# Two-branch gated mix on one core: subtractions and products of the feature maps move from VectorE to GpSimd, 131 instead of 130 packs of softmax exponentials on VectorE, and a new planned order

## The chip, the cores and the metric

The kernel runs on one core of a Trainium2 chip. Its engines are TensorE (PE; matmuls, and PEld for the loads of their weights), VectorE (DVE), ScalarE (ACT), GpSimd (POOL) and SyncE (SP, which here only issues DMAs). The metric is the device time of one execution in microseconds; the kernel before takes 737.42 us, the median of 3 runs (737.13 to 737.89).

## The reference

Two attention branches share the input `x` (2048 tokens, 512 features, 32 heads of 16) and are mixed by a gate of each token:

```python
x = A_x
g = _sigmoid((x * gate_w).sum(-1, keepdims=True))
# branch A: softmax attention
q, k, v = split(x @ A_wqkv)                       # 32 heads of 16
p = softmax(einsum("bhqd,bhkd->bhqk", q, k) * 16 ** -0.5)
a = (p @ v) @ A_wo
# branch B: linear attention with "hedgehog" feature maps
q, k, v = split(x @ B_wqkv)
pq, pk = q @ w_phi, k @ w_phi                     # 16x16 per head
phi_q = concat([softmax(pq), softmax(-pq)])       # 32 features
phi_k = concat([softmax(pk), softmax(-pk)])
kv = einsum("bhsf,bhsd->bhfd", phi_k, v);  z = phi_k.sum(over s)
b = (einsum("bhqf,bhfd->bhqd", phi_q, kv) / (phi_q . z + 1e-6)) @ B_wo
return g * a + (1 - g) * b
```

Branch A needs 2048 x 2048 x 32 exponentials. They are the bulk of the work.

## The kernel before, in words

**Units, packs, groups.** A unit is one head, 128 keys and 512 queries: one score matmul into a PSUM bank (128 x 512) and one exponential of it. Four units of four heads make a pack (512 packs in all), 16 packs (all keys) a group, of which there are 32, eight for each of the four stretches of 512 queries.

**Two ways to an exponential.** Most units go to ScalarE: `_qk` (the matmuls of `_scores`, L1131) fills 2 or 3 banks of a ring of five, and `_exp` (L1183) makes the exponentials of these 2 or 3 banks in one instruction, into `ET`. The packs named in `AWAY` (one number for each group; bit n stands for key block 1 + 3n, and bit 5, if it were set, for pack 510, the second last of all) go to VectorE: `_vector_bits` turns each of the four score banks into a bit pattern (L962, `va`, "v_bits"), and `_vector_terms` makes three shifted copies out of it that stand for a sum of powers of two; the first is `va` itself or a shift of it on VectorE (L984, `vp`, "v_term", one or two packs in one instruction), and the third is made by GpSimd in two halves (`_pool_term`, L999, "p_term"). `_values` (L1250) multiplies `ET`, or the terms, with the values. A vector pack costs 12 such matmuls where a pack of ScalarE costs 4. `_fill` (L1257) adds zeros where PE would otherwise run dry.

**End of a group.** `_norm` moves the accumulated 128 x 512 tile out of PSUM by a transpose (L1271, "n_t1", into `T1`) and, after every second group, makes the factor from the softmax's denominator and the gate (L1278 on GpSimd, L1280), multiplies (L1282, "n_mul", from `T1` into `T2`) and sends the result through two DMAs (`turned`, then `onTA`) to the output matmuls. The last group has a function of its own, `_norm_last`, which works by halves.

**Branch B.** It is worked off beside the attention, by four token tiles of 128 at a time (`_b_quad`, called eight times: four for the keys, four for the queries). Each call projects (L651, L1395), finds the greatest and the least of each head's 16 values by a tree (L1414, "b_max"), subtracts each from the values (L1423, "b_sub", two instructions of 128 x 2048 in a quad), lets ScalarE make the two exponentials (L1425, "b_exp"), sums them (L1430, L1432, and L1434 on GpSimd) and scales one side by a ratio (`_b_scale`: L1447 to L1455, of which "b_mul", 128 x 2048, is L1450 for keys and L1455 for queries). The keys' product is read by the `kv` matmuls (L1473), the queries' by transposing DMAs (L1511).

**What sets the order.** The order on each engine is fixed when the program is built. Every operation is given to a planner (`Plan.op`) with an engine, a cost and a due time (`prio`); `Plan.order` places them one by one, first what can start earliest, then what is due first, and writes one list for each engine. `SHIFT` moves the due times of tagged groups of operations by up to 14 packs. Operations named in `PORT` and all of GpSimd's are placed so that they don't overlap: each GpSimd operation is made to wait for the latest VectorE operation of that kind, while VectorE is not made to wait for GpSimd's. Each engine then works its list strictly in order and waits at each entry for semaphores. ScalarE's list holds the exponentials of both branches, so an L1425 whose input is late stops the L1183 behind it.

Of the kernel before, what the change touches and what calls it, by code (L numbers as in the profile page):

```python
# [7 lines left out]
ALU = mybir.AluOpType  # L8
AX = mybir.AxisListType

P = 128
# [378 lines left out]
class _Kernel:  # L390
# [364 lines left out]
    def _gate(self):  # L755
# [44 lines left out]
    AWAY = (26, 27, 26, 31, 22, 13, 15, 15, 31, 15, 13, 31, 30, 23, 31, 15, 29, 31, 26, 27, 31, 26, 31, 21, 31, 31, 28, 31, 31, 11, 23, 31)  # L800

    SHIFT = (
# [582 lines left out]
    def _b_quad(self, s, t0, due):  # L1385
# [22 lines left out]
        def run(name, cost, fn, at, reads, writes):  # L1408
            eng = "POOL" if name in ("b_ratio", "b_tot") else "DVE"
            op(eng, fn, cost, reads=reads, writes=writes, name=name, prio=due + gap * at)  # L1410
# [259 lines left out]
```

## Time and profile before

| | |
|---|---|
| median of 3 runs | 737.42 us (737.13 to 737.89) |
| profiled execution | 737.4 us, of which the span of the profile is 735.6 us |
| granted TensorE clock | 1.000 |
| PE, DVE, ACT, POOL busy | 713.1, 690.5, 723.5, 303.8 us |
| exponentials of branch A on ACT | 304 of 128 x 1536, 303 of 128 x 1024, a few smaller |
| score tiles turned by DVE (L962) | 520, which is 130 packs |

Busy time is the time in which at least one instruction of the engine was running; instructions of one engine overlap by their ends, so the mean durations times the count exceed the busy time. "Idle before" and the waits name what an engine waited for. Times within the profile count from the span's start.

### The profile page before, as it was taken

What the parts mean: (1) busy time and instruction counts of PE and PEld (TensorE: products, weight loads), DVE (VectorE), ACT (ScalarE), POOL (GpSimd) and SP (SyncE); (2) the same over time, 40 slices, a digit from 0 to 9 for tenths busy, and PEclk for the clock granted to TensorE, in tenths of its full rate; (3) what the DMA queues carried; (4) which work ended last, traced back from release to release, by engine and by line L of the source; (5) the groups of instructions that cost most, each with busy time, mean ns of one, the idle gap of its engine ahead of it and who ended that gap; (6) DMA issues with size and microseconds to landing.
All of it is one profiled execution on the core that took longest, in us unless ns stands there. A gap on an engine that the chain in (4) does not pass through costs nothing.

```text
span 735.6 us, 19777 instructions
## 1 busy us (share of the span) xinstructions
PE 713.1 (97%) x8549; PEld 234.4 (32%) x8549; DVE 690.5 (94%) x1085; ACT 723.5 (98%) x636; POOL 303.8 (41%) x318
## 2 busy tenths in 40 slices
PE   8999999999999999999999999999999999999998
PEld 3334233243223223332232233333332233332322
DVE  4899999988999999999999999999999999999996
ACT  6999999999999999999999999999999999999996
POOL 3832342424544424535353344334334444344442
PEclk9999999999999999999999999999999999999999
DMA  9400100001010010100001032042123111003210
GB/s 201 145 10 6 22 2 9 16 4 18 4 15 11 4 20 2 17 11 8 14 2 17 15 61 28 8 83 35 23 45 74 21 16 23 16 25 63 40 29 30
DMA packets 90041, 21.96 MB, mean 30 GB/s; under 512 B 82913, under 2 KB 89441, under 8 KB 89953
## 3 DMA queue, kind: packets, MB, share of 16 engines
q1 hardware_dynamic: 88752, 20.30, 14.5%
q8 instruction: 67, 1.10, 0.7%
q10 hardware_dynamic: 1200, 0.39, 0.2%
q14 instruction: 22, 0.17, 0.1%
HBM read 4.21 MB, written 2.10 MB: 9 GB/s over the span
## 4 chain that ended last, share of the span: by engine, by line
ACT 73%; PE 13%; DVE 11%; DMA 1%; issue 0%; POOL 0%; DVEq 0%; POOLq 0%
ACT ET L1183 70%; PE ps L1131 5%; DVE va L962 4%; PE ps L1250 4%; ACT bq L1425 3%; PE ps L651 2%; DVE vp L984 2%; DVE btree L1414 1%; DMA xT<-in_A_x_dram 1%; PE ps L744 1%; PE ps L1257 1%; DVE bq L1423 0%; DVE VB L1541 0%; DVE nb L1541 0%; DVE rb L1539 0%
## 5 line engine op out<-in xcount | busy, mean ns | idle before, releaser
L1183 ACT ACTIVATE ET<-ps 128x1536 bf16<-128x1536 f32 (+1 forms) x612 | 692.9, 1343 | 4.6 <-PE ps L1131 4.4
L999 POOL TENSOR_SCALAR vp<-va 128x1024 uint16<-128x1024 uint16 x264 | 275.7, 1044 | 337.3 <-DVE vp L984 124.2
L962 DVE TENSOR_SCALAR va<-ps 128x512 uint16<-128x512 f32 x520 | 339.5, 681 | 23.9 <-PE ps L1131 21.7
L1131 PE MATMUL ps<-qT,kT 32*128 32x512 bf16 (+1 forms) x2053 | 311.0, 384 | 10.1 <-ACT ET L1183 5.1
L1131 PEld LDWEIGHTS ps<-qT,kT 32*128 32x128 bf16 x2053 | 82.7, 91 | 258.3 <-ACT ET L1183 146.5
L984 DVE TENSOR_SCALAR vp<-va 128x4096 uint16<-128x4096 uint16 (+1 forms) x151 | 162.0, 1079 | 0.6 <-PE ps L1250 0.2
L1250 PE MATMUL ps<-ET,V 128*32 128x512 bf16 x1532 | 149.0, 385 | 1.3 <-DVE T L1271 1.0
L1250 PE MATMUL ps<-vp,vc 128*32 128x512 bf16 x1040 | 93.9, 384 | 0.3 <-DVE vp L984 0.2
L1250 PEld LDWEIGHTS ps<-ET,V 128*32 128x32 bf16 x1532 | 39.3, 95 | 64.9 <-issue 48.6
L651 PE MATMUL ps<-WB,xT 128*32 128x512 bf16 x768 | 57.4, 382 | 0.5 <-DVE bq L1395 0.3
L1250 PE MATMUL ps<-va,V 128*32 128x512 bf16 x520 | 51.3, 385 | 0.0
L1250 PE MATMUL ps<-vp,V 128*32 128x512 bf16 x520 | 48.2, 383 | 0.3 <-DVE vp L984 0.2
L1257 PE MATMUL ps<-kT,zero 128*32 128x512 bf16 x468 | 42.1, 384 | 0.0
L651 PE MATMUL ps<-xT,WA 128*32 128x512 bf16 x480 | 36.1, 382 | 0.6 <-DVE va L962 0.4
L1250 PEld LDWEIGHTS ps<-vp,vc 128*32 128x32 bf16 x1040 | 24.7, 95 | 35.3 <-issue 20.2
L1425 ACT ACTIVATE bq<-bq 128x2048 bf16<-128x2048 bf16 x16 | 31.5, 1989 | 0.1
L1271 DVE STREAM_TRANSPOSE T<-ps 128x512 f32<-128x512 f32 x31 | 21.9, 708 | 1.1 <-PE ps L1250 1.0
L651 PE MATMUL ps<-WoB,WT 128*32 128x512 bf16 x256 | 22.6, 383 | 0.3 <-DVE va L962 0.3
L1395 DVE CAST bq<-ps 128x512 bf16<-128x512 f32 x32 | 21.7, 678 | 0.3 <-PE ps L651 0.2
L651 PEld LDWEIGHTS ps<-WB,xT 128*32 128x32 bf16 x768 | 15.2, 95 | 19.9 <-issue 10.4
L651 PE MATMUL ps<-WoA,onTA 128*32 128x512 bf16 x256 | 21.2, 381 | 0.0
L744 PE MATMUL ps<-WA,xT 128*128 128x128 bf16 x256 | 19.5, 220 | 0.7 <-DVE va L962 0.4
(94 smaller groups left out, 367.1 us busy)
## 6 DMA issues: line engine op xcount, KB each, us to landing
turned<-T SPq DMA_DIRECT2D x240, 8.0 KB, 1.8
qT<-qs SPq DMA_DIRECT2D x120, 16.0 KB, 1.8
WB<-in_B_wqkv_dram SPq DMA_DIRECT2D x1, 1536.0 KB, 6.9
out_dram<-WB SPq DMA_DIRECT2D x12, 128.0 KB, 2.0
WA<-in_A_wqkv_dram SPq DMA_DIRECT2D x3, 384.0 KB, 5.1
WoA<-in_A_wo_dram SPq DMA_DIRECT2D x1, 512.0 KB, 8.0
WoB<-in_B_wo_dram SPq DMA_DIRECT2D x1, 512.0 KB, 8.9
out_dram<-xT SPq DMA_DIRECT2D x3, 128.0 KB, 1.8
```

The lines of the kernel that those rows point to most:

```text
L651: ins = e.matmul(out[32 * g:32 * g + 32], lhs[:, 32 * g:32 * g + 32], rhs, start=start, stop=stop, tile_position=(0, 32 * g), skip_group_c ...
L744: ins = e.matmul(self._bank(job)[:, P * tt:P * tt + P], self.xT[:, c, QCH * j + TOK * tt:QCH * j + TOK * tt + TOK], self.WA[:, 2, c, P * c ...
L962: parts.append(op("DVE", lambda e, j=j, job=job: e.tensor_scalar(self.va[:, pair, side, j, :], self._bank(job), SCALE * LOG2E * 128.0, (12 ...
L984: self.plan.op("DVE", lambda e, k=k, shift=shift: e.tensor_scalar(flat(self.vp[:, k]), flat(self.va[:, pair]), float(shift), None, op0=ALU ...
L999: o = self.plan.op("POOL", lambda e, flat=flat: e.tensor_scalar(flat[0], flat[1], 1.0, float(shift), op0=ALU.mult, op1=ALU.add), 0.08 + n ...
L1131: return e.matmul(out, self.kT[32 * i:32 * i + 32, cp, kt * TOK:(kt + 1) * TOK], self.qT[32 * i:32 * i + 32, s, at], start=True, stop=True ...
L1183: o = plan.op("ACT", lambda e: e.activation(self.ET[:, a % NS:a % NS + n, at], self.ps[:, self._ring(a):self._ring(a) + n, at], ACT.Exp, s ...
L1250: ins = e.matmul(self._bank(ot)[32 * i:32 * i + 32, at], V[:, v0:v0 + 32], tile(), start=(kt == 0), stop=(kt == self.NT - 1), tile_positio ...
L1257: ins = e.matmul(self._bank(ot)[32 * i:32 * i + 32, :], self.zero[:], self.kT[:, 0, 0:QCH], start=False, stop=False, tile_position=(0, 32 ...
L1271: self.turned_out = op("DVE", lambda e: e.transpose(T1[:, side].rearrange("p b s -> p (b s)"), src()), 0.635, deps=last, writes=[b_T1[side ...
L1395: [lambda e, b, k=k: e.tensor_copy(bq[:, k].rearrange("p (g s v) -> p g s v", g=8, s=2)[:, :, 0, :], b.rearrange("p (g v) -> p g v", g=8))],
L1425: op("ACT", lambda e, side=side: e.activation(sides[side], sides[side], ACT.Exp, scale=1.0 - 2 * side), self.c_act(2048) + 0.04, reads=[bu ...
```

## The change

`b_sub`, `b_mul` and `n_mul` go from VectorE to GpSimd. `b_sub` and `b_mul` are cut in two halves of 128 x 1024 each, and the planner is given 1.52 for a half; for `n_mul` it is given 0.31 + 0.3 n, with n the number of groups (2, once 1). `_norm_last` keeps its product on VectorE. `AWAY` names 131 packs instead of 130, among them pack 510, and `SHIFT`, and with it the whole order on every engine, is another. By stretches of 512 queries the vector packs are 29, 33, 34 and 35 (before 29, 34, 32 and 35); they form 59 pairs and 13 singles (before 54 and 22).

```diff
-    AWAY = (26, 27, 26, 31, 22, 13, 15, 15, 31, 15, 13, 31, 30, 23, 31, 15, 29, 31, 26, 27, 31, 26, 31, 21, 31, 31, 28, 31, 31, 11, 23, 31)
+    AWAY = (22, 27, 13, 23, 23, 22, 30, 30, 29, 15, 27, 31, 30, 23, 27, 15, 15, 31, 23, 31, 13, 27, 31, 15, 27, 31, 31, 27, 15, 31, 14, 47)
     SHIFT = (
...
@@ _norm
-        op("DVE", lambda e: e.tensor_tensor(
+        op("POOL", lambda e: e.tensor_tensor(
             T2[:].rearrange("p b (s d) -> p s b d", s=2)[:, lo:hi], T1[:, lo:hi, :, 0:16],
-            rinv[:, lo:hi, :, None].to_broadcast([P, n, 16, 16]), ALU.mult), 0.065 + 0.269 * n,
+            rinv[:, lo:hi, :, None].to_broadcast([P, n, 16, 16]), ALU.mult), 0.31 + 0.3 * n,
            reads=reads + [b_rinv], writes=[b_T2], name="n_mul", prio=due)
@@ _b_quad
-            eng = "POOL" if name in ("b_ratio", "b_tot") else "DVE"
+            eng = "POOL" if name in ("b_sub", "b_ratio", "b_tot", "b_mul") else "DVE"
...
-            run("b_sub", two(2048), lambda e, out=out, t=t: e.tensor_tensor(out, p, spread(t[:, :, 0], 32), ALU.subtract),
-                at, [pos, tree[side]], [buf])
+            for a in (0, 16):
+                run("b_sub", 1.52, lambda e, a=a, out=out, t=t: e.tensor_tensor(
+                    out[:, a:a + 16], p[:, a:a + 16], spread(t[:, a:a + 16, 0], 16), ALU.subtract),
+                    at, [pos, tree[side]], [buf])
@@ _b_scale
-                    ("b_mul", two(2048), lambda e: e.tensor_tensor(x[:, 0::2], x[:, 0::2], spread(r, 32), ALU.mult),
-                     b_r + both, [both[0]])]
+                    *[("b_mul", 1.52, lambda e, a=a: e.tensor_tensor(
+                        x[:, a:a + 32:2], x[:, a:a + 32:2], spread(r[:, a // 2:a // 2 + 16], 16), ALU.mult),
+                       b_r + both, [both[0]]) for a in (0, 32)]]
...
-                ("b_mul", two(2048), lambda e: e.tensor_tensor(x[:, 1::2], x[:, 1::2], spread(r, 32), ALU.mult),
-                 b_r + both, [both[1]])]
+                *[("b_mul", 1.52, lambda e, a=a: e.tensor_tensor(
+                    x[:, a + 1:a + 32:2], x[:, a + 1:a + 32:2], spread(r[:, a // 2:a // 2 + 16], 16), ALU.mult),
+                   b_r + both, [both[1]]) for a in (0, 32)]]
```

207 rows, old and new, of the table SHIFT are left out of this document.

## The prediction

> **What bounds the kernel now.** I read the page's head and its chain first, then who ScalarE (ACT) waited for, then busy time by stretch of 25 us, then the merged chain in order of time.
>
> ```profile
> span 735.6 us, 19777 instructions
> ...
> PE 713.1 (97%) x8549; PEld 234.4 (32%) x8549; DVE 690.5 (94%) x1085; ACT 723.5 (98%) x636; POOL 303.8 (41%) x318
> ...
> ACT 73%; PE 13%; DVE 11%; DMA 1%; issue 0%; POOL 0%; DVEq 0%; POOLq 0%
> ```
>
> ```profile
> ACT ET L1183 <- PE ps L1131: 4.4, 1, 4.4
> ACT xT L1619 <- PE ps L651: 2.9, 1, 2.9
> ACT L1183 <- issue: 1.8, 1, 1.8
> ```
>
> ```profile
> 50.00:75.00 25.00, 24.01 (x294) 10.87 (x292) 23.03 (x40) 24.89 (x24) 5.26 (x6) 1.00 0.06 8
> ...
> 525.00:550.00 25.00, 24.60 (x318) 8.51 (x315) 24.33 (x47) 24.91 (x22) 8.36 (x8) 1.00 0.22 35
> ...
> sum 750.00, PE 713.12 PEld 234.43 DVE 690.45 ACT 723.53 POOL 303.79; mean PE 23.77 PEld 7.81 DVE 23.02 ACT 24.12 POOL 10.13
> ```
>
> Three engines look nearly full, but only one has no idle time in the middle. ACT's three waits are one at the start (4.4 us), one in front of it (1.8) and one at the end (2.9). The columns of the third fence are the stretch, then the busy time of PE, PEld, DVE, ACT and POOL; the two stretches are the worst for ACT between 25 and 725 us, and they lack 0.11 and 0.09 us of 25. So from the first exponential to the last the time is the sum of ACT's instructions, and a change shortens this stretch only by taking work from ACT. DVE's 94% and POOL's 41% bound nothing by themselves.
>
> ACT's own pace and its ends:
>
> ```profile
> 69.45 40.78 ACT ET L1183 x36
> ...
> 113.96 1.79 ACT bq L1425
> ```
>
> ```profile
> 688.80 37.52 ACT ET L1183 x33
> ...
> 731.68 1.18 ACT xT L1619 x2
> ```
>
> 36 exponentials, 2 and 3 banks by turns, take 40.78 us: 1.133 each, 2.266 for a pair (5 units), 0.453 a unit. The last begins before 726.33; what follows, 9.3 us, is PE's last matmuls, the last output copies and the store.
>
> **The change, part by part.**
>
> *One more pack for DVE (ACT's load).* 1528 of 2048 units are ACT's now (520 are DVE's), 1524 after.
>
> ```profile
> L1183 ACT ACTIVATE ET<-ps 128x1536 bf16<-128x1536 f32 x304 | 473.7, 1558 | 0.2
> L1183 ACT ACTIVATE ET<-ps 128x1024 bf16<-128x1024 f32 x303 | 344.8, 1138 | 0.0
> ...
> L1070 ACT ACTIVATE ET<-ps 128x768 bf16<-128x768 f32 x2 | 1.7, 872 | 0.0
> ...
> L1070 ACT ACTIVATE ET<-ps 128x256 bf16<-128x256 f32 x2 | 0.9, 432 | 0.0
> ```
>
> The two forms differ by 0.420 us for 512 columns, 0.82 ns a column. A pair has 2560 columns, 2.10 of its 2.266 us, so an instruction adds 0.083 us beyond its columns. By the alternation in `_exp`, 1528 units leave one instruction of three and one of a single unit over, which 1524 don't: two instructions and 2048 columns go, 0.166 + 1.68 = 1.85 us. In `_last_pack` the ring position is now a multiple of five, so its 768 + 256 columns, twice, become 1024, twice: two instructions fewer, up to 0.17 us, of which I take 0.05, since the tail is PE's. ACT: **-1.9 us**. This is on the path.
>
> *What DVE loses and gains (off the path).*
>
> ```profile
> 473.48 1.13 DVE bq L1423
> ...
> 492.06 1.20 DVE va L962 x2
> ```
>
> ```profile
> L1423 DVE TENSOR_TENSOR bq<-bq,btree 128x2048 bf16<-128x2048 bf16 x16 | 19.8, 1239 | 0.0
> ...
> L1455 DVE TENSOR_TENSOR bq<-bq,brec 128x2048 bf16<-128x2048 bf16 x4 | 4.8, 1212 | 0.0
> ```
>
> ```profile
> 115.18 0.68 DVE L1282 TENSOR_TENSOR T<-T,rinv 128x512 bf16<-128x512 f32 x1
> 115.78 0.68 DVE L750 CAST V<-ps 128x512 bf16<-128x512 f32 x1
> ```
>
> 16 `b_sub` at 1.13 are 18.1 us; 8 `b_mul`, of a like mean duration, 9.0; 15 `n_mul` at 0.60 (start to next start) 9.0. Four more score tiles at 0.60 add 2.4. The shifts barely move: 54 pairs and 22 singles become 59 and 13. DVE: about -34 us, to 657. No wait of ACT names DVE, so I cost this gain at nothing.
>
> *What GpSimd gains.* No half of 1024 with two inputs is in the trace. The nearest rows:
>
> ```profile
> L999 POOL TENSOR_SCALAR vp<-va 128x1024 uint16<-128x1024 uint16 x264 | 275.7, 1044 | 337.3 <-DVE vp L984 124.2 <-DVE va L962 90.5 <-PE ps L1250 69.7
> ...
> L1278 POOL TENSOR_TENSOR rinv<-T,gh 128x32 f32<-128x32 f32 x15 | 5.0, 333 | 7.4 <-DVE vp L984 2.6 <-DVE T L1271 2.3 <-DVE btree L1430 1.2
> L1434 POOL TENSOR_TENSOR bsum<-btree 128x256 f32<-128x256 f16 x8 | 4.9, 612 | 31.3 <-DVE vp L984 15.1 <-DVE btree L1432 11.1 <-DVE T L1282 5.0
> ...
> L1448 POOL TENSOR_TENSOR bsum<-bsum,VB 128x128 f32<-128x128 f32 x4 | 2.1, 518 | 0.7 <-DVE VB L1447 0.5
> ```
>
> From 128 to 256 columns the slope is 94/128 = 0.73 ns, from 32 to 128 it is 185/96 = 1.93, and over the whole 32 to 256 it is 279/224 = 1.25. Carried on from 612 at 256, a half takes 1.18, 2.09 or 1.57 us. I take 1.57, the chord over all rows, which the code's own 1.52 is near; both ends stay for the range. 48 halves are 75 us, 15 `n_mul` at 612 + 256 x 1.25 = 0.93 are 14, two more terms 2.1: POOL goes from 304 to about 395 us, 54%. It stands idle 337 us in front of its terms, which is the cover.
>
> The Trainium skill ("GPSIMD Engine Reference", section 3.1) puts a two-input elementwise operation at about 2.6 cycles an element; at 1.2 GHz a half would be 2.22 us (an estimate from that page), above even my upper end. No row here has 1024 columns and two inputs, so the trace can't refuse it; the sum with it stands at the third rival.
>
> *Latency.* A quad's `b_sub` grows from 1.13 to 2 x 1.57 = 3.14 us and its `b_mul` likewise. `b_sub` is what matters: the exponential behind it stands in ACT's list in a fixed place.
>
> ```profile
> 543.59 1.14 DVE bq L1423
> 544.75 1.91 ACT bq L1425
> ```
>
> ```profile
> 122.32 1.21 DVE L1423 TENSOR_TENSOR bq<-bq,btree 128x2048 bf16<-128x2048 bf16 x1
> ```
>
> ```profile
> 124.72 1.94 ACT L1425 ACTIVATE bq<-bq 128x2048 bf16<-128x2048 bf16 x1
> ```
>
> In the first fence the chain runs through `b_sub` into ACT: the L1425 starts as its input is ready, and this is the 0.09 us that the stretch 525 to 550 lacks. So a late `b_sub` is paid by ACT at once. With the new order the planner puts the exponential at 2 x 1.52 and a wake-up behind the tree; 1.57 against 1.52 makes 0.1 us for a pair of halves where the place is tight, up to 16 x 0.1 = 1.6 us were all tight. The other two rows show one that wasn't: it starts 1.19 us after its `b_sub`'s end. So some have slack, and the rest of the list can run ahead, so I take 0 and keep 1.6 as the end. `b_mul` is read by the `kv` matmuls or the transposing DMAs of the same quad, `n_mul` by a DMA and then by the next group but one's turn: quads lie 49 to 64 packs (735.6/512 = 1.4 us each) apart, pairs of groups 32 packs, so 2 us more have tens of us of cover; cost 0, and up to 0.3 us at the last pair, which is near the end.
>
> *The shared pair of ports.* A shift of VectorE and an operation of GpSimd don't run together:
>
> ```profile
> 93.97 2.17 POOL L999 TENSOR_SCALAR vp<-va 128x1024 uint16<-128x1024 uint16 x2 [6.75 <-PE ps L1250]
> ```
>
> ```profile
> 87.54 1.20 DVE L984 TENSOR_SCALAR vp<-va 128x4096 uint16<-128x4096 uint16 x1
> 95.60 1.62 DVE L984 TENSOR_SCALAR vp<-va 128x4096 uint16<-128x4096 uint16 x1
> ```
>
> The first shift runs alone, the second starts while POOL is at work until 96.14 and takes 0.42 us longer. A half of 1.57 can hold VectorE longer than a term of 1.04. Bounds: 0, and 48 x 1.57 = 75 us of VectorE. By the row seen, 48 x 0.42 = 20 us, inside the 34 freed. Cost on the path 0.
>
> *PE* gets 8 more matmuls for the pack (12 terms for 4), 16 of which take 0.98 us, so 0.5 us; L1257's fillers, put in where PE is short of work, cover it:
>
> ```profile
> 517.98 0.98 PE ps L1250 x16
> ```
>
> ```profile
> L1257 PE MATMUL ps<-kT,zero 128*32 128x512 bf16 x468 | 42.1, 384 | 0.0
> ```
>
> *New order, pack 510.* It may shift the start (ACT's 4.4 us wait for the first keys) and the tail by some tenths either way; what it does to ACT's fill in the middle can't be seen beforehand. I take 0.
>
> **Sum**: the profiled execution takes 737.4 us (span 735.6, 1.8 around it), as the median 737.42 does; 737.4 - 1.9 = **735.5 us**, -0.26%. Since 0.2% (1.5 us, about what a measurement of this kernel can tell from no change) lies at 735.9, 0.4 us of new idle time is enough to make it "the same".
>
> **The rivals.**
>
> *1. Same: the new order isn't quite full.* ACT's list has over 600 entries, and the planner's times are not the chip's. For it: the 1.6 us above; PE stands close to its limit. Against it: the order before lost some 0.2 us in the middle. Idle of 0.4 to 3.4 us gives 735.9 to 738.9.
>
> *2. Slower: ACT waits for `b_sub`.* Sixteen times, two GpSimd operations, each behind whatever stands before them in POOL's list, separate the tree from an exponential that blocks ACT. If each finds on average half of one unplanned operation in front (0.55 us, from 1.04 or 1.13), that is 16 x 0.55 = 8.8 us: 744.3. It decides from 1.9/16 = 0.12 us a time on; slower by 0.2% from 0.21. For it: the chain at 543.59, where even VectorE's single `b_sub` was just in time. Against it: POOL has idle time before most of its work, and the places are new.
>
> *3. Slower: the halves cost more than the plan's 1.52.* At the upper row bound, 2.09, each pair is 1.14 us late: 16 x 1.14 = 18 us, 753.7 us. By the Trainium skill's figure above it would be 16 x 1.4 = 22 us, 758 us. Against it: 256 columns of two inputs take 0.612 us, start-up and all.
>
> *4. Slower: PE waits for terms that stand behind the halves.*
>
> ```profile
> PEld ps L1250 <- POOL vp L999: 2.2, 8, 0.5
> ```
>
> Now 8 waits, 0.5 at most. A half in front makes a term 1.57 later; the ring hides about one exponential (1.13), so 0.44 us a time: 8 times 3.5 us (739.0), at all 32 `b_sub` halves 14 (749.6).
>
> **How the numbers follow.** As summed 0.43, 735.0 to 735.9; a better start or tail besides, below 735.0, 0.05; rival 1 0.20; rival 2 0.20; rival 3 0.06; rival 4 0.06. Faster 0.48, same 0.20, slower 0.32. The range goes from 734.5 to 744.5: rival 3, the dearer parts of 2 and 4, and a few hundredths below are left out, under 2 in 10. The likeliest case's own range is 735.0 to 735.9.
>
> **What would show it.** Right: 303 of each of ACT's two large forms instead of 304 and 303; its waits again only at the ends; DVE near 657 us, POOL near 395; halves of 1.5 to 1.6 us; span near 733.7. Wrong: a wait of ACT's L1425 for a POOL line (rival 2, or 3 if the halves exceed 1.7 us); waits of PE's L1250 for L999 well over 2.2 us, with ACT's L1183 waiting for PE (rival 4); small waits of L1183 for PE alone (rival 1).

## The result and the profile after

The changed kernel takes 748.91 us (median of 6 runs, 748.18 to 752.18) against 737.65 (6 runs, 737.13 to 738.21): a ratio of 1.0161, 95% interval 1.0151 to 1.0171. It is slower by 1.6%, where 735.5 us and "faster" were forecast; 748.9 lies above the range's end of 744.5.

Its page (head, busy times, chain by engine; the profiled execution took 749.03 us):

```profile
span 747.0 us, 19911 instructions
...
PE 716.8 (96%) x8610; PEld 234.6 (31%) x8610; DVE 683.1 (91%) x1041; ACT 725.2 (97%) x632; POOL 418.2 (56%) x384
...
PE 46%; ACT 25%; DVE 22%; POOL 6%; issue 1%; DVEq 0%
```

The chain was 73% ACT before; now it is 25%, and the time is handed round between PE, VectorE and GpSimd. The granted clock is 1.000 as before, so the loss isn't the clock's. ACT's own waits (engine, line, for whom: us in total, times, longest):

```profile
ACT ET L1182 <- PE ps L1130: 10.1, 15, 4.9
ACT bq L1426 <- POOL bq L1423: 3.0, 7, 0.8
ACT xT L1622 <- PE ps L651: 2.9, 1, 2.9
ACT L1182 <- issue: 1.8, 1, 1.8
ACT ET L1069 <- PE ps L1130: 0.5, 1, 0.5
```

4.9 of the first row is the start (4.4 before); the other 14 waits, 5.2 us, and the 7 waits of the feature maps' exponentials for the subtraction (3.0 us) are new. Groups of instructions (count, busy us and mean ns of one, idle time in front):

```profile
L1182 ACT ACTIVATE ET<-ps 128x1536 bf16<-128x1536 f32 x303 | 465.1, 1535 | 5.2 <-PE ps L1130 4.6
L983 DVE TENSOR_SCALAR vp<-va 128x4096 uint16<-128x4096 uint16 x117 | 156.1, 1342 | 0.4 <-PE ps L1249 0.2
L1182 ACT ACTIVATE ET<-ps 128x1024 bf16<-128x1024 f32 x303 | 337.1, 1113 | 0.6 <-PE ps L1130 0.6
L1423 POOL TENSOR_TENSOR bq<-bq,btree 128x1024 bf16<-128x1024 bf16 x32 | 61.7, 1928 | 37.7 <-DVE vp L983 30.6 <-DVE btree L1413 6.3
...
L1451 POOL TENSOR_TENSOR bq<-bq,brec 128x1024 bf16<-128x1024 bf16 x8 | 16.4, 2044 | 4.0 <-DVE vp L983 2.4 <-DVE brec L1450 1.3
L1281 POOL TENSOR_TENSOR T<-T,rinv 128x512 bf16<-128x512 f32 x15 | 15.8, 1056 | 13.5 <-DVE rinv L1279 8.7 <-DVE vp L983 3.4 <-DVE btree L1413 1.1
L1457 POOL TENSOR_TENSOR bq<-bq,brec 128x1024 bf16<-128x1024 bf16 x8 | 15.3, 1916 | 1.1 <-DVE vp L983 0.7
```

A half takes 1.92 to 1.93 us (medians; one of L1451 took 2.93, hence the mean of 2044 ns) and a gate product 1.06, not the 1.52 and 0.91 for which the lists were made. ACT's instructions are 303 of each large form, as forecast. Their means are shorter than before (1535 for 1558, 1113 for 1138), and in e8_half_8 below, where ACT hardly waits, they are longer (1583, 1163). I read this as short gaps between neighbours, which then overlap less, so that a part of the loss doesn't show as idle time: ACT's busy time rose by 1.7 us although 1.9 us of work went. The waits of PE for GpSimd:

```profile
PEld ps L1249 <- POOL vp L998: 11.1, 16, 1.5
...
PE ps L1249 <- POOL vp L998: 5.8, 9, 1.2
```

Before there were 8 such waits of the weight loads (PEld), 2.2 us together, and none of the matmuls (PE). The two rows cover the same stretches, so they don't add. One quad shows both ways of the loss (GpSimd's, then ACT's instructions in order of time: start, us, what):

```profile
198.35 1.93 POOL L1423 TENSOR_TENSOR bq<-bq,btree 128x1024 bf16<-128x1024 bf16 x1 [1.29 <-DVE vp L983]
200.36 1.04 POOL L998 TENSOR_SCALAR vp<-va 128x1024 uint16<-128x1024 uint16 x1
201.49 1.93 POOL L1423 TENSOR_TENSOR bq<-bq,btree 128x1024 bf16<-128x1024 bf16 x1
203.50 1.04 POOL L998 TENSOR_SCALAR vp<-va 128x1024 uint16<-128x1024 uint16 x1
```

```profile
203.45 1.91 ACT L1426 ACTIVATE bq<-bq 128x2048 bf16<-128x2048 bf16 x1 [0.70 <-POOL bq L1423]
```

GpSimd works without a wait from 198.35 on; the second half ends at 203.42, and ACT starts its exponential at 203.45 after 0.70 us of waiting. Two halves of 1.52 us would have ended 0.82 us earlier, which is more than this wait. The terms of L998 behind the first and the second half are later by 0.41 and 0.82 us than they would be behind such halves.

### The profile page after: what moved, and what is told of

The parts are those of the page before. It is cut to its first block, busy times and chain, and to the rows that moved or that the text cites. A ratio compares the mean times of both kernels' runs of the same rounds, so it can differ in the third digit from the quotient of the medians.

```text
span 747.0 us, 19911 instructions
## 1 busy us (share of the span) xinstructions
PE 716.8 (96%) x8610; PEld 234.6 (31%) x8610; DVE 683.1 (91%) x1041; ACT 725.2 (97%) x632; POOL 418.2 (56%) x384
## 4 chain that ended last, share of the span: by engine, by line
PE 46%; ACT 25%; DVE 22%; POOL 6%; issue 1%; DVEq 0%
ACT ET L1182 24%; PE ps L1130 17%; PE ps L1249 15%; DVE va L961 9%; PE ps L651 8%; DVE vp L983 6%; POOL vp L998 3%; DVE btree L1413 2%; POOL bq L1423 2%; PE ps L1256 2%; PE ps L744 1%; DVE btree L1431 1%; DVE T L1270 1%; DVE btree L1433 1%; PE ps L643 1%
## 5 line engine op out<-in xcount | busy, mean ns | idle before, releaser
L1182 ACT ACTIVATE ET<-ps 128x1536 bf16<-128x1536 f32 (+1 forms) x610 | 692.3, 1320 | 10.7 <-PE ps L1130 10.1
L998 POOL TENSOR_SCALAR vp<-va 128x1024 uint16<-128x1024 uint16 x266 | 282.8, 1063 | 195.2 <-DVE vp L983 73.4
L983 DVE TENSOR_SCALAR vp<-va 128x4096 uint16<-128x4096 uint16 (+1 forms) x143 | 176.0, 1240 | 1.7 <-PE ps L1249 1.4
L1249 PE MATMUL ps<-ET,V 128*32 128x512 bf16 x1528 | 147.2, 385 | 1.2 <-DVE T L1270 1.1
L1249 PE MATMUL ps<-vp,vc 128*32 128x512 bf16 x1040 | 95.6, 385 | 6.8 <-POOL vp L998 5.8
L1423 POOL TENSOR_TENSOR bq<-bq,btree 128x1024 bf16<-128x1024 bf16 x32 | 61.7, 1928 | 37.7 <-DVE vp L983 30.6
L1249 PEld LDWEIGHTS ps<-ET,V 128*32 128x32 bf16 x1528 | 39.0, 95 | 63.1 <-issue 47.1
L1249 PE MATMUL ps<-va,V 128*32 128x512 bf16 x524 | 51.6, 385 | 0.1
L1249 PE MATMUL ps<-vp,V 128*32 128x512 bf16 x524 | 49.4, 383 | 0.6 <-DVE vp L983 0.5
L1256 PE MATMUL ps<-kT,zero 128*32 128x512 bf16 x520 | 46.4, 384 | 0.2 <-DVE V L750 0.2
L1249 PEld LDWEIGHTS ps<-vp,vc 128*32 128x32 bf16 x1040 | 24.8, 95 | 45.8 <-issue 23.0
L1281 POOL TENSOR_TENSOR T<-T,rinv 128x512 bf16<-128x512 f32 (+1 forms) x16 | 16.5, 1029 | 16.6 <-DVE rinv L1279 11.8
L651 PE MATMUL ps<-WoA,onTA 128*32 128x512 bf16 x256 | 23.0, 382 | 0.0
L651 PE MATMUL ps<-WoB,WT 128*32 128x512 bf16 x256 | 22.5, 382 | 0.3 <-DVE va L961 0.2
```

Of the source, the lines that this page charges most:

```text
L651: ins = e.matmul(out[32 * g:32 * g + 32], lhs[:, 32 * g:32 * g + 32], rhs, start=start, stop=stop, tile_position=(0, 32 * g), skip_group_c ...
L983: self.plan.op("DVE", lambda e, k=k, shift=shift: e.tensor_scalar(flat(self.vp[:, k]), flat(self.va[:, pair]), float(shift), None, op0=ALU ...
L998: o = self.plan.op("POOL", lambda e, flat=flat: e.tensor_scalar(flat[0], flat[1], 1.0, float(shift), op0=ALU.mult, op1=ALU.add), 0.08 + n ...
L1182: o = plan.op("ACT", lambda e: e.activation(self.ET[:, a % NS:a % NS + n, at], self.ps[:, self._ring(a):self._ring(a) + n, at], ACT.Exp, s ...
L1249: ins = e.matmul(self._bank(ot)[32 * i:32 * i + 32, at], V[:, v0:v0 + 32], tile(), start=(kt == 0), stop=(kt == self.NT - 1), tile_positio ...
L1256: ins = e.matmul(self._bank(ot)[32 * i:32 * i + 32, :], self.zero[:], self.kT[:, 0, 0:QCH], start=False, stop=False, tile_position=(0, 32 ...
```

## The experiments

Three theories. **L**: the halves are 0.40 us longer than the plan that the lists were made from, and the lists have no room for it. **P**: GpSimd's work of this amount holds VectorE's ports too often, whatever was planned. **O**: the new order, or the 131st pack, is bad by itself.

### Length of the halves, the lists unchanged

```diff
-                run("b_sub", 1.52, lambda e, a=a, out=out, t=t: e.tensor_tensor(
-                    out[:, a:a + 16], p[:, a:a + 16], spread(t[:, a:a + 16, 0], 16), ALU.subtract),
+                run("b_sub", 1.52, lambda e, a=a, out=out, t=t: e.tensor_tensor(
+                    out[:, a:a + 12], p[:, a:a + 12], spread(t[:, a:a + 12, 0], 12), ALU.subtract),
...
-                        x[:, a:a + 32:2], x[:, a:a + 32:2], spread(r[:, a // 2:a // 2 + 16], 16), ALU.mult),
+                        x[:, a:a + 24:2], x[:, a:a + 24:2], spread(r[:, a // 2:a // 2 + 12], 12), ALU.mult),
```

The gate product likewise covers 13 of its 16 blocks; the columns left out are set once. This is e7_half_12; e8_half_8 takes 8 of 16 everywhere, e9_sub_12 shortens the subtractions alone, e10_mul_12 the scalings and gate products alone.

> The lists of the changed kernel; each half of the subtractions and scalings covers 12 of its 16 groups of 64 columns, and the gate products 13 of their 16 blocks (the rest is left out), with one instruction as in the change. By the durations measured (0.612 us at 256 columns, 1.92 at 1024) a half should take 1.49 us, a gate product 0.89: the plan's 1.52 and 0.91. Theory L (what costs is what the operations exceed their planned time by): 735 to 738 us, all of the loss and the 131st pack's gain come out. Theory P (GpSimd's time as such holds VectorE's ports): a quarter of the loss goes, 745 to 747. Theory O (the order or the pack): 747 or more.

Measured: 736.98 us, ratio 0.9998 (0.9978 to 1.0017; one of the ten runs took 743.5).

> As e7_half_12 with 8 of 16 groups and blocks: 1.05 us a half, 0.61 a gate product, well below the plan. L: nothing more to win, 734.5 to 737, within a few tenths of e7. P: the loss goes on falling with GpSimd's time, to about half of the change's, 742. O: 747 or more.

Measured: 736.34 us, ratio 0.9978 (0.9969 to 0.9988).

> As e7_half_12, but only the subtractions are shortened; the scalings and gate products keep their full length. If the loss sits with the subtractions (ScalarE's exponential behind them, and the terms that queue behind them): 736 to 739. If each GpSimd operation costs by its excess over the plan (subtractions 32 x 0.40 of 21.5 us): 740 to 741.

Measured: 740.72 us, ratio 1.0048 (1.0029 to 1.0067).

> As e7_half_12, but only the scalings and gate products are shortened. Loss with the subtractions: 746 to 749. By excess (8.7 of 21.5 us): 743 to 744.

Measured: 746.08 us, ratio 1.0110 (1.0095 to 1.0125).

The halves of e7_half_12 and of e8_half_8, and the waits in e7_half_12 of ACT and of PE for GpSimd's terms:

```profile
L1427 POOL TENSOR_TENSOR bq<-bq,btree 128x768 bf16<-128x768 bf16 x32 | 47.7, 1492 | 38.4 <-DVE vp L983 32.7 <-DVE btree L1415 4.8
```

```profile
L1427 POOL TENSOR_TENSOR bq<-bq,btree 128x512 bf16<-128x512 bf16 x32 | 33.8, 1056 | 40.7 <-DVE vp L983 34.8 <-DVE btree L1415 5.1
```

```profile
ACT ET L1182 <- PE ps L1130: 5.9, 3, 4.7
ACT xT L1626 <- PE ps L651: 2.9, 1, 2.9
ACT L1182 <- issue: 1.8, 1, 1.8
ACT ET L1069 <- PE ps L1130: 0.5, 1, 0.5
```

```profile
PE ps L1249 <- POOL vp L998: 0.6, 2, 0.4
...
PEld ps L1249 <- POOL vp L998: 3.2, 10, 0.7
```

With the same lists and the same packs, halves of the planned length give back 11.9 us, all of the loss (11.3) and a little more: ACT's wait for the subtraction is gone, and so are all but two of its waits for PE behind the start. Theory O falls. So does P as it was put, that the loss goes with GpSimd's time: GpSimd is still busy 390.5 us (53%), and going on to halves of 1.06 us, another 26 us less of GpSimd's work, brings only 0.6 us more, while the step from 1.93 to 1.49, 28 us, brought 11.9. The knee at the planned length is what L expects.

It is also where ACT is full again, so the knee alone doesn't say by which way the excess reached ACT. The matmuls' waits of L1249 for GpSimd's terms went from 5.8 to 0.6 us; but VectorE's busy time fell with the halves too, from 683.1 to 669.7 us. How much of the loss went through GpSimd's own list, and how much through VectorE being held up beside longer halves, these runs don't separate.

The subtractions carry most of it: shortening them alone gives 8.2 us, the scalings and gate products alone 2.8. ACT's wait for the subtraction is gone in e9_sub_12 and still 3.0 us in e10_mul_12. By microsecond of GpSimd's work that is 8.2/(32 x 0.433) = 0.59 for the subtractions and 2.8/(16 x 0.50 + 15 x 0.16) = 0.27 for the rest.

### A miss that went the other way

> The lists of every engine as in the changed kernel, but each GpSimd half and each gate product is made in two shorter instructions, a two-input one on a part of the columns and a one-input copy on the rest, so that together they should take about the 1.52 us (0.91 for the gate product) that the plan was given, instead of the 1.92 (1.06) measured. What is left out: the subtraction, the scaling and the gate product of the copied columns. Theory L (the halves are 0.40 us longer than the order was made for, and that is what costs): 735 to 738 us. Theory P (any GpSimd work of this amount holds VectorE's ports too often, whatever its planned length): the stalls shrink only with GpSimd's time, by a quarter of 13 us, 745 to 747. Theory O (the new order or the 131st pack is what is bad): 748 to 749, no change.

```diff
+                run("b_sub", 1.52, [lambda e, a=a, out=out, t=t: e.tensor_tensor(
+                    out[:, a:a + 5], p[:, a:a + 5], spread(t[:, a:a + 5, 0], 5), ALU.subtract),
+                    lambda e, a=a, out=out: e.tensor_scalar(
+                    out[:, a + 5:a + 16], p[:, a + 5:a + 16], 1.0, None, op0=ALU.mult)],
```

Measured: 795.69 us, ratio 1.0784 (1.0702 to 1.0866). The one-input copy was to be cheap and wasn't:

```profile
L1427 POOL TENSOR_SCALAR bq<-bq 128x704 bf16<-128x704 bf16 x32 | 68.5, 2142 | 0.0
...
L1430 ACT ACTIVATE bq<-bq 128x2048 bf16<-128x2048 bf16 x16 | 30.6, 1910 | 22.5 <-POOL bq L1427 22.5
L1425 POOL TENSOR_TENSOR bq<-bq,btree 128x320 bf16<-128x320 bf16 x32 | 25.2, 787 | 29.5 <-DVE vp L983 22.5 <-DVE btree L1415 5.7
```

0.79 + 2.14 make 2.93 us a half, so this run is roughly a fourth point of the same curve, on its far side: 1.06, 1.49, 1.93 and 2.93 us a half give 736.3, 737.0, 748.9 and 795.7 us. ACT now waits 22.5 us for the subtraction alone, and the granted clock fell to 0.951, which before stood at 1.000; what part of the loss the clock has, wasn't separated.

### The operations back on VectorE, the lists unchanged

```diff
             p.order()
+            moved = [o for o in p.queues["POOL"] if o.name in ("b_sub", "b_mul", "n_mul")]
+            for o in moved:
+                o.eng = "DVE"
+            p.queues["POOL"] = [o for o in p.queues["POOL"] if o.eng == "POOL"]
+            p.queues["DVE"] = sorted(p.queues["DVE"] + moved, key=lambda o: o.start)
```

> The lists of the changed kernel, but after the planning all 64 moved operations are taken out of GpSimd's list and put into VectorE's at the place that their planned start gives them. L: the order itself is good and VectorE makes a half in about 0.6 us, so 735 to 739, unless VectorE gets too full at these places. P: the same, since the port conflict goes. O: 748 or more, as the order and the 131 packs stay.

Measured: 762.84 us, ratio 1.0340 (1.0308 to 1.0373).

> As e2, but only the 32 halves of the subtraction go back to VectorE; the scaling and the gate products stay on GpSimd. If the waits of ScalarE for late subtractions and the terms that queue behind them are most of the loss (rival 2 and 4 by way of the subtraction): 736 to 740. If all GpSimd operations cost alike, by their planned excess (32 of 48 halves at 0.40 and 15 products at 0.15: 12.8 of 21.5 us): 740 to 742.

Measured: 752.70 us, ratio 1.0210 (1.0193 to 1.0227), with only "b_sub" in the list of names.

Both missed the ranges of L and P. The waits of ACT in e2_dve_place:

```profile
ACT ET L1187 <- PE ps L1135: 28.6, 31, 4.7
ACT xT L1627 <- PE ps L656: 2.9, 1, 2.9
```

I had taken the changed kernel's VectorE, 34 us less loaded than before by my count, for a list with room. Measured, it is only 7.4 us less busy than before (683.1 for 690.5), and there is no room at these places: what is put in delays what stands behind it, and PE and ACT with it. The granted clock of the profiled execution was 0.982 in e2_dve_place, which may have a part in its loss, but 0.998 in e5_sub_on_dve. Alone these two runs would have spoken for O; e7_half_12, with the same order and packs, rules that out.

> The lists of the kernel before (130 packs), but after the planning the 16 subtractions, 8 scalings and 15 gate products (uncut) are taken out of VectorE's list and put into GpSimd's by their planned start. No place was made for their length here. L: much slower than the change, since each subtraction is 2 x 1.92 - 1.13 = 2.7 us later than its exponential's place: 16 x 2.7 = 43 us at most, 755 to 780. O: about the old time, 737 to 742, since the order and the pack count are the old ones.

```diff
             p.order()
+            moved = [o for o in p.queues["DVE"] if o.name in ("b_sub", "b_mul", "n_mul")]
+            for o in moved:
+                o.eng = "POOL"
...
+            p.queues["POOL"] = sorted(p.queues["POOL"] + moved, key=lambda o: o.start)
```

Measured: 811.62 us, ratio 1.0994 (1.0957 to 1.1030), beyond even L's upper end. In the old lists, made for 1.13 us on VectorE, a whole subtraction takes 3.98 us on GpSimd (the granted clock was 0.939 here, which may have a part in this loss too):

```profile
ACT ET L1188 <- PE ps L1136: 42.3, 46, 4.4
ACT bq L1430 <- POOL bq L1428: 26.7, 14, 2.8
```

### Can the work be carried at its true length?

> The changed kernel with the true lengths told to the planner (1.95 for a half, 0.18 + 0.44 n for a gate product) and SHIFT and AWAY left as they are, so that the planner places everything anew. If knowing the price is enough: 736 to 738. If SHIFT fits one plan only and is worth nothing for another: far slower, 770 to 800.

```diff
-                run("b_sub", 1.52, lambda e, a=a, out=out, t=t: e.tensor_tensor(
+                run("b_sub", 1.95, lambda e, a=a, out=out, t=t: e.tensor_tensor(
...
-            rinv[:, lo:hi, :, None].to_broadcast([P, n, 16, 16]), ALU.mult), 0.31 + 0.3 * n,
+            rinv[:, lo:hi, :, None].to_broadcast([P, n, 16, 16]), ALU.mult), 0.18 + 0.44 * n,
```

Measured: 797.16 us, one run. Mending the price and keeping the shifts made it worse. That `SHIFT` fits one plan only, and pushes at the wrong operations in another, is the likeliest reading of it; what else differs between the two orders wasn't taken apart.

> The operations of the changed kernel, whole and on the same engines (131 packs, all three kinds on GpSimd at their true length), but every list rearranged by small moves until, in the planner's own bookkeeping with 1.97 us for a half and 1.09 for a gate product (start to next start), ScalarE has no gaps, also when VectorE's and GpSimd's durations scatter by 3%. If the loss is only that the order was made for a wrong length (theory L): 736 to 737.5, 0 to 0.2% faster than before, as e7 and e8. If GpSimd at this length can't carry the work in any order (too slow, or too much in VectorE's way): 742 or more.

```diff
             p.order()
+            self._repair(p)
...
+            ops = [o for e in p.ENGS for o in p.queues[e]]
...
+                p.queues[e] = [ops[at + k + by[at + k]] for k in range(n)]
```

`by` is a table of displacements (nearly all within some tens of places).

Measured: 746.74 us, ratio 1.0119 (1.0104 to 1.0134).

> The same with another outcome of the rearrangement, to see how far one order stands for others: the same expectations as for the first, and the two within 1.5 us of each other if L holds.

Measured: 752.94 us (five runs, 749.71 to 759.01; a sixth took 763.46), ratio 1.0227 (1.0189 to 1.0265).

Both missed L's 736 to 737.5, in both directions from 748.9, and lie 6 us from each other where 1.5 was expected. In the bookkeeping ACT had no gaps; on the chip it has, for PE, and PE's matmuls wait for VectorE's "v_bits" (L1008 here) more than for GpSimd's terms (L1045). Of the first of the two:

```profile
ACT ET L1229 <- PE ps L1177: 14.6, 13, 4.3
...
ACT L1229 <- issue: 1.8, 1, 1.8
```

```profile
PE ps L1177 <- DVE va L1008: 8.1, 23, 1.3
...
PE ps L1296 <- POOL vp L1045: 0.5, 1, 0.5
```

In the changed kernel the waits of PE for these two lines were 3.7 and 5.8 us. So these lists took GpSimd's terms out of PE's way and left PE waiting for VectorE. Two of its stretches of 25 us (the third column from the end is the granted clock):

```profile
675.00:700.00 25.00, 23.19 (x239) 6.77 (x236) 24.10 (x35) 24.50 (x22) 16.82 (x14) 0.96 0.36 61
700.00:725.00 25.00, 24.46 (x253) 7.09 (x250) 21.84 (x41) 22.11 (x20) 12.30 (x12) 0.83 0.18 33
```

In two places the clock sinks, to 0.91 (475 to 500 us) and here to 0.83, and ACT lacks 3 us each time. That may be part of the loss, not all of it: from 325 to 350 us ACT lacks 1.4 us at a clock of 1.00. By the words written before the run, 742 or more would mean that GpSimd at this length can't carry the work in any order. Two orders in which the clock sank as well don't show that, and they don't show L's other half either, that a right plan would be enough. Whether some order carries GpSimd's work at its true length at 736 us stays open.

> The lists of the changed kernel, with whole results: of the 32 groups of each subtraction and scaling GpSimd makes 12 and 12, so that a half takes the 1.49 us of e7_half_12, and VectorE makes the last 8 (128 x 512, estimated at 0.33 us, a quarter of the 1.13 to 1.21 that the whole took there) in 24 new operations, put into its list at the planned start of the first half. The gate products stay at 1.06. If only GpSimd's excess matters and VectorE has room: 737 to 739. If VectorE's list has no room either, as e5_sub_on_dve and e2_dve_place suggest (about 0.7 us of the run for each 1 us added to VectorE): 8 us more on VectorE make 742 to 745.

```diff
-            for a in (0, 16):
-                run("b_sub", 1.52, lambda e, a=a, out=out, t=t: e.tensor_tensor(
-                    out[:, a:a + 16], p[:, a:a + 16], spread(t[:, a:a + 16, 0], 16), ALU.subtract),
-                    at, [pos, tree[side]], [buf])
+            run("b_sub", 1.52, sub(0, 12), at, [pos, tree[side]], [buf])
+            run("b_sub", 1.52, (sub(12, 24), sub(24, 32)), at, [pos, tree[side]], [buf])
```

(The second of a pair is what VectorE makes; `b_mul` likewise.)

Measured: 754.32 us, ratio 1.0210 (1.0185 to 1.0235), beyond both expectations; the granted clock of the profiled execution was 0.984. VectorE's new operations, and one of them beside GpSimd's half:

```profile
L1440 DVE TENSOR_TENSOR bq<-bq,btree 128x512 bf16<-128x512 bf16 x16 | 19.0, 1186 | 0.1
...
L1465 DVE TENSOR_TENSOR bq<-bq,brec 128x512 bf16<-128x512 bf16 x8 | 7.9, 993 | 0.1
```

```profile
111.94 1.33 DVE L1440 TENSOR_TENSOR bq<-bq,btree 128x512 bf16<-128x512 bf16 x1
```

```profile
111.50 1.49 POOL L1440 TENSOR_TENSOR bq<-bq,btree 128x768 bf16<-128x768 bf16 x1 [1.47 <-DVE btree L1431]
```

Another, begun just ahead of its half:

```profile
188.32 0.43 DVE L1440 TENSOR_TENSOR bq<-bq,btree 128x512 bf16<-128x512 bf16 x1
```

```profile
188.37 1.73 POOL L1440 TENSOR_TENSOR bq<-bq,btree 128x768 bf16<-128x768 bf16 x1 [2.22 <-DVE btree L1431]
```

VectorE's pieces take 1.19 and 0.99 us on the mean, not 0.33, where the kernel before makes a tree step of the same size in 0.44:

```profile
L1414 DVE TENSOR_TENSOR btree<-btree 128x512 bf16<-128x512 bf16 x16 | 7.1, 444 | 0.0
```

The place was mine: at the planned start of GpSimd's half, where both ask for the ports. The piece begun at 111.94 ends at 113.27, 0.28 us after the half begun at 111.50 (it ended at 112.99). The piece begun at 188.32 takes 0.43 us, and then the half is the one that takes longer, 1.73 instead of 1.49 us. Of the 24 pieces, 18 were of the first kind and 6 of the second. The Trainium skill ("SBUF — State Buffer", section "SBUF: two separate sides") calls the shared pair of ports an exclusive lock that the one of the two that starts first holds for its whole instruction; the trace agrees in both directions. So 24 pieces made 27 us of VectorE instead of 8. This cost by the ports is real, but here it came from my edit. In e7_half_12 the large shifts take 1268 ns on the mean, 1342 in the changed kernel, 1237 before.

## Why the prediction was wrong

- **The sum's frame held.** ACT was the bound, the pack and the last pack's rounding are worth about 1.9 us: 303 + 303 instructions came, and with halves shorter than planned (e8_half_8) ACT is busy 721.1 us, 2.4 less than before, and the profiled execution has a span of 733.6 us where 733.7 was forecast for the change. The median of that run, 736.34, is 0.8 us above the 735.5; about half of this lies outside the span (2.2 to 2.3 us instead of the 1.8 before).
- **The step that failed is the price of a half.** "I take 1.57, the chord over all rows" should have been 1.92, inside the bounds of 1.18 and 2.09 that stood beside it. Across 512, 768 and 1024 columns the runs show 1056, 1492 and 1928 ns: 1.70 ns a column and 0.18 us at the start. This line gives 0.62 us at 256 columns, where the row of before had 0.612, but 0.24 and 0.40 at 32 and 128, where the rows had 0.333 and 0.518: the small rows lie above it, and they flattened the chord. The rows that I showed also mixed types (two F32 inputs at 128 and 32 columns, one f16 and an F32 output at 256). I overlooked one of bf16, the type of the halves (least, median and greatest duration in ns, then the times of the first and the last):

```profile
L588 POOL TENSOR_TENSOR bq<-wphi,head x2: 612/612/613, 19.3 to 19.9; 128x256 bf16<-128x256 bf16 x2
```

It takes the same 612 ns as the f16 row, so at 256 columns the type wasn't what misled. That the code's 1.52 lay near the chord made the chord look right. But a planner's cost in the code is a claim, not a measurement, and the trace of before had no two-input row above 256 columns to test it on.
- **The Trainium skill** ("GPSIMD Engine Reference", section 3.1) gave an estimate of 2.22 us for a half. Measured is 1.92; the page was nearer than my chord. At the page's 1.2 GHz, 1.70 ns are 2.0 cycles a column for bf16, against the page's 2.6 for fp32.
- **Rival 3 was the right one and got 0.06.** Its own formula at the measured length, 16 x 2 x (1.92 - 1.52) = 12.8 us on 735.5, gives 748.3 for the 748.9 measured. That it comes so near is luck: the formula counts the subtractions alone and at their full excess, and by e9_sub_12 and e10_mul_12 these are worth 8.2 us and the scalings and gate products, which it leaves out, 2.8. Its path, too, is only part of what happened: ACT waited for the subtraction itself 3.0 us. More of the excess went the way of rival 4, through terms that stood behind the halves (the weight loads' waits of L1249 for L998 went from 2.2 to 11.1 us, the matmuls' from none to 5.8), and reached ACT as waits of L1182 for PE (5.2 us behind the start) and as the short gaps that the means of L1182 show. Rival 2's unplanned operations aren't needed: at the planned length no wait of ACT for a GpSimd line is left (e7).
- **"Some have slack, and the rest of the list can run ahead, so I take 0"** failed with it. The subtractions' halves, 0.433 us longer than in e9_sub_12, make 13.9 us together, and 8.2 of them, 59%, were paid: the lists absorbed 41%, not all. I read ACT's place behind one subtraction (1.19 us of slack) from the old order; the new order was packed anew for 1.52, so that slack in the old one didn't carry over.
- **VectorE's relief**: 657 us forecast, 683.1 measured. Its operations take longer beside GpSimd's: the large shifts 1342 ns instead of 1237, which for 117 of them is 12 of the 26 us (an estimate), and the last step of the "b_max" tree 455 instead of 227, another 4. The rest wasn't taken apart. As forecast, this relief had no worth of its own, but neither was it there to spend (e2, e5, e12).
- **GpSimd**: 395 forecast, 418.2 measured; 48 x 0.35 = 17 us of the difference is the price of the halves.

## What to carry to other kernels

A fixed order made from costs is worth as much as its dearest wrong cost: before such a change, measure the moved operation alone, in its own type and size, and compare it with the number in the plan. Where a price must be carried on from smaller rows, look for all rows of its type, start from the largest, and give the steepest slope a chance that fits what hangs on it: here 0.4 us, 48 times, in a list without gaps. And to find whether an order or a duration is to blame, keep the lists and change the duration: that one run cleared the order and the extra pack, which moving operations between lists could not.

## What the runs showed of the hardware

- GpSimd's two-input operation on bf16: 0.18 us and 1.70 ns a column from 512 to 1024 columns (1056, 1492 and 1928 ns at 512, 768 and 1024). The medians at 1024 are 1916 to 1928 ns in the changed kernel, whether it subtracts or multiplies.
- GpSimd's TENSOR_SCALAR with one operation on 704 bf16 columns in runs of 64 takes 2.14 us (e1_planned_length), while the two-operation form takes 1.04 us for 1024 contiguous uint16 columns (before). Whether the missing second operation, the type or the strides cost it wasn't tried.
- A VectorE operation with two inputs (128 x 512, bf16) that starts with more than 0.6 us of a GpSimd operation still to run ends 0.28 us after it, in 18 of 18 cases of e12_split (it takes 0.92 to 1.70 us). Begun up to 0.1 us ahead of a half, it takes 0.39 to 0.43 us, and the half 1.67 to 1.74 instead of 1.49 (6 of 6).
- The granted clock was 1.000 in the profiled executions of the kernel before and of the change. It was 0.951 in e1_planned_length and sank in single stretches to 0.91 and 0.83 in e11_repaired_1. Whether PE's stalls brought it down or it brought the stalls wasn't separated.
